# Queries stored beside the state: one product for keys by state and keys by queries in a delta-rule kernel

## The chip, the cores and the metric

The kernel runs on one core of one Trainium2 chip. The metric is the device time of one execution in microseconds, and the median of several executions is compared. Below, PE is TensorE (PEld its weight loads), DVE is VectorE, ACT is ScalarE, POOL is GpSimd and SP is SyncE.

## The reference

The kernel computes a linear attention with the delta rule, and feeds its result to a feed-forward layer with a PReLU whose slope differs by channel. There are B = 4 batches, H = 8 heads, S = 768 positions and a head size of D = 48; the feed-forward layer has 3072 tokens, a width of 384 and an inner width of 2048. All of it is fp32.

```python
k_n = k / (norm(k, axis=-1) + 1e-06)
state = zeros((B, H, D, D))
for t in range(S):
    kt, vt, bt = k_n[:, :, t], v[:, :, t], beta[:, :, t, None]
    y[:, :, t] = einsum('bhd,bhde->bhe', q[:, :, t], state)
    v_old = einsum('bhde,bhd->bhe', state, kt)
    state = state + bt[..., None] * einsum('bhd,bhe->bhde', kt, vt - v_old)
x = y.transpose(0, 2, 1, 3).reshape(B * S, H * D)
h = x @ w_in
g = maximum(h, 0.0) + alpha * minimum(h, 0.0)
out = g @ w_out
```

## The kernel before

**Chunks and steps.** Positions are taken in chunks of C = 64. A step n is one chunk for two of the four batches, so there are 12 x 2 = 24 steps, and steps n and n+2 belong to the same two batches and to the same state tile `state[bp]`. Within a chunk the recurrence is written as a triangular system. A step needs these products, each as 16 small matmuls, one for every combination of head pair g (4), head parity a (2) and batch t (2), in the order that `quarters()` gives:

- `grams(n_k, n_q)`: keys by keys for a later step n_k (L386, the triangular matrix), or keys by queries for step n_q (L386, then the mask `minus` on VectorE at L403, which gives `a_t`).
- `through_state(n)`: keys by state and queries by state (L672), both into one PSUM tile. VectorE subtracts the first from the scaled values (L675, the right-hand side `r`), ACT copies the second (L680, `y`).
- `between_1`, `between_2` (L629, L644): the off-diagonal block of the inverse.
- `solve(n)` (L686): inverse by right-hand side, scaled on VectorE (L690, `u`).
- `outputs(n)` (L699): `a_t` by `u`, added to `y` on VectorE (L706).
- `next_state(n)` (L715): keys by `u`, subtracted from the state by two VectorE instructions (L721).
- `flips` (L353) transposes keys and queries on TensorE, and ACT copies them to `k_t` and `q_t` (L375). `to_ffn` (L730, L732) transposes `y` for the feed-forward layer.

The operands of one small matmul lie in one half of the partitions (`dims(a)`: 48 rows from 0 or 64), and its output goes to one half of the PSUM partitions, so the four combinations of a and t use the four quarters of the array.

**Other work on VectorE.** The inverse of the 32-wide diagonal blocks is made by elimination for four steps at a time (L463 to L476, and transposes at L446). It is woven into the steps n with n % 4 < 3, as long as n < 20. The feed-forward layer needs L829 (ACT) and L831 (two VectorE instructions) for each bank of its first product, and sums of operands (L773) for a fast form of its second product (`ffn_out_fast`, L883).

**Order.** The instruction order of every engine is written out by hand. `weave` advances several generators in proportion to their lengths. From step 4 on, one step is `attention(n)` with four shares, between which matmuls of the feed-forward layer of an earlier chunk are placed (L819, first product; L883, second product):

1. `place(n+1)`, `through_state(n)`, `between_1(n+1)`
2. `solve(n)`, the key grams of step n+8, `between_2(n+1)`, scaling of v
3. `outputs(n)`, `next_state(n)`, the query grams of step n+1, loads
4. `flips` (keys of step n+9, queries of step n+2), `to_ffn(n)`, loads

Steps 0 and 1 have no state yet; `queries()` makes their query products. Steps 2 and 3 run together in `ready(2)` and `pair(2)`: there the query grams of both come in `ready`, and the state products of both stand back to back in `pair`. Step 4 is prepared by `prelude`.

**PSUM.** `ps_big()` hands out tiles of two banks from a ring of three. A request waits until every reader of the tile handed out three requests earlier is done. Two further banks (`p_ffn`) alternate for the feed-forward layer.

Of the kernel before, what the change touches and what calls it, by code (L numbers as in the profile page):

```python
# [25 lines left out]
FP32 = mybir.dt.float32  # L26
# [15 lines left out]
def kernel(  # L42
# [29 lines left out]
    def ps_big():  # L72


        return psum.tile([128, 2, 512], FP32, name="p_big", tag="big", bufs=3)
# [215 lines left out]
        nc.tensor.transpose(p, al_sb, ident[:FT, :FT])  # L291
        nc.scalar.activation(al_t, p, ACT.Copy, scale=-1.0, bias=1.0)

    state = [const.tile([128, 2, G, D], FP32, name=f"state{bp}") for bp in range(NB)]

    NE = 2
    diag = [const.tile([128, H, C], FP32, name=f"diag{i}") for i in range(NE)]
# [61 lines left out]
    def flips(n_k, n_q):  # L359

        both = n_k < N and n_q < N
        p = ps_big() if both else None
        copies = []
        if n_k < N:
            p_k = p[:, 0] if both else ps_one()
            flip(early(n_k), p_k)
            k_t[n_k] = work.tile([128, G, 128], FP32, name="k_t", bufs=EARLY + 1)
            copies.append((k_t[n_k], p_k))
        if n_q < N:
            p_q = p[:, 1] if both else ps_one()  # L370
            flip(q_pad[n_q % NQ], p_q)
            q_t[n_q] = work.tile([128, G, 128], FP32, name="q_t")
            copies.append((q_t[n_q], p_q))
        for dst, src in copies:
            nc.scalar.copy(dst.rearrange("p g i -> p (g i)"), src)  # L375

    def quarters():
        return [(g, a, t) for g in range(G) for a in range(2) for t in range(2)]

    def grams(n_k, n_q):  # L380

        p = ps_big().rearrange("p a (w g i) -> p a w g i", w=2, g=G)
        for w, n, rhs in ((0, n_k, k_t), (1, n_q, q_t)):
            if n < N:
                for g, a, t in quarters():
                    nc.tensor.matmul(  # L386
                        p[half(t ^ a if w else t), a, w, g], k_t[n][dims(a), g, half(t)],
                        rhs[n][dims(a), g, half(t)],
                    )
        if n_k < N:  # L390
            w = stats[n_k][1][:, 0:2, :, None].to_broadcast([128, 2, G, HB])
            for dst, cols in (
                (gather(n_k), slice(0, HB)), (right[n_k % EARLY][:, 1:], slice(HB, C))
            ):
                nc.vector.tensor_tensor(  # L395
                    out=dst.rearrange("p (a g) i -> p a g i", a=2), in0=p[:, :, 0, :, cols],
                    in1=w, op=ALU.mult,
                )
            keep(n_k)

        if n_q < N:
            a_t[n_q] = work.tile([128, H, C], FP32, name="a_t")
            nc.vector.tensor_tensor(  # L403
                out=a_t[n_q].rearrange("p (a g) i -> p a g i", a=2), in0=p[:, :, 1],
                in1=minus[:, None, None, :].to_broadcast([128, 2, G, C]), op=ALU.mult,
            )

# [253 lines left out]
    def through_state(n):  # L663
        c, bp = steps[n]
        if c == 0:
            rhs_[n] = by_parity(nv[n])
            return
        r = work.tile([128, H, D], FP32, name="r")
        p = ps_big()[:, :, 0 : 2 * G * D].rearrange("p a (w g d) -> p a w g d", w=2, g=G)
        for w, x in ((0, k_t), (1, q_t)):  # L670
            for g, a, t in quarters():
                nc.tensor.matmul(  # L672
                    p[half(t), a, w, g], x[n][dims(a), g, half(t)], state[bp][dims(a), t, g]
                )
        nc.vector.tensor_tensor(  # L675
            out=r.rearrange("p (a g) d -> p a g d", a=2), in0=by_parity(nv[n]), in1=p[:, :, 0],
            op=ALU.subtract,
        )
        y = work.tile([128, H, D], FP32, name="y")
        nc.scalar.copy(by_parity(y), p[:, :, 1])  # L680
        rhs_[n], ys[n] = r.rearrange("p (a g) d -> p a g d", a=2), y

    def solve(n):
        p = ps_big()[:, :, 0 : G * D].rearrange("p a (g d) -> p a g d", a=2, g=G)
# [271 lines left out]
    def attention(n):  # L956


        place(n + 1, (0,))
        through_state(n)  # L960
        between_1(n + 1)
        yield
        solve(n)
        grams(n + EARLY, N)
        between_2(n + 1)
        scale_v(n + 1)
        yield
        outputs(n)
        next_state(n)
        grams(N, n + 1)  # L970
        load_late(n + 2)
        squares(n + EARLY + 1)
        yield
        flips(n + EARLY + 1, n + 2)
        to_ffn(n)
        weigh(n + EARLY + 1)
        load_early(n + EARLY + 1 + NKE)
        load_q(n + 3)
        load_v(n + 3)
        yield  # L980
# [34 lines left out]
    def ready(n):  # L1015

        both = (n, n + 1)
        for i in both:
            place(i, (0,))
            flips(N, i)  # L1020
            load_q(i + 2)
        yield
        for i in both:
            between_1(i)
        yield
        for x in (1, 2, 3):
            for i in both:
                place(i, (x,))
        for i in both:
            grams(N, i)  # L1030
        yield
        for i in both:
            between_2(i)
            scale_v(i)
            yield

    def queries():

        p = [x.rearrange("p (n g i) -> p n g i", n=2, g=G) for x in ffn_banks]
        for n in range(2):  # L1040
            for g, a, t in quarters():
                nc.tensor.matmul(
                    p[a][half(t ^ a), n, g], k_t[n][dims(a), g, half(t)],
                    q_t[n][dims(a), g, half(t)],
                )
            a_t[n] = work.tile([128, H, C], FP32, name="a_t")

        def mask(n):
            for a in range(2):
                nc.vector.tensor_tensor(  # L1050
                    out=a_t[n][:, a * G : (a + 1) * G], in0=p[a][:, n],
                    in1=minus[:, None, :].to_broadcast([128, G, C]), op=ALU.mult,
                )

        return mask
# [48 lines left out]
    def statics(first, last):  # L1104
        if first > 0:
            squares(first)
        for n in range(first, last + 1):
            if n < last:
                squares(n + 1)
            weigh(n)  # L1110
            flips(n, N)
            yield
            if n > 0:
                load_early(n + NKE)
            if n > first:
                grams(n - 1, N)
            yield
        grams(last, N)
        yield


# [99 lines left out]
    def prelude(n):  # L1221
        place(n)
        yield
        between_1(n)
        yield
        between_2(n)
        yield
        grams(N, n)
        scale_v(n)
        yield  # L1230

    def catch_up():
        for n in range(FIRST + NJ, EARLY + NJ):
            grams(n, N)
            flips(n + 1, N)
            squares(n + 1)
            yield
            weigh(n + 1)
            load_early(n + 1 + NKE)
            yield  # L1240
# [65 lines left out]
```

## Time and profile before

| What | Value |
|---|---|
| Median of 5 runs | 686.56 us (686.35 to 687.33) |
| The profiled execution | 686.98 us, of it a span of 685.1 us in the profile |
| TensorE busy | 665.5 us (97%), 10063 matmul records |
| TensorE weight loads | 573.7 us (84%) |
| VectorE busy | 462.2 us (67%), 1133 instructions |
| ScalarE busy | 248.7 us (36%), 592 instructions |
| DMA | 37.76 MB, mean 55 GB/s |
| Granted TensorE clock | 0.999 |

The state products (L672) have 704 + 704 records, that is 22 steps of 16 + 16 matmuls with two records each; the query grams (L386) have 704. The records of a matmul overlap with those of its neighbours, so the time of a group is read from the start of the group to the start of the next one, not from the mean duration. Step n's state products start at 80.15 us for the pair of steps 2 and 3, at 155.54 for step 4, 170.17 for 5, 186.21 for 6, 214.48 for 7, and then every 25 to 26 us, until 619.26 for step 23. After 642 us only the feed-forward layer of the last chunk is left.

In a line of the timeline the columns are: start, duration, engine, line and operation, output and inputs, number of instructions merged, and in brackets the idle time before it with what ended it.

### The profile page before, as it was taken

How to read it: one execution, taken by the hardware profiler on the slowest of the kernel's cores; microseconds unless marked ns; L12 is line 12 of the kernel's file. 1: busy time of each engine (PE TensorE's matmuls, PEld its weight loads, DVE VectorE, ACT ScalarE, POOL GpSimd, SP SyncE). 2: the span in 40 equal slices, each digit the busy share in tenths (PEclk: the TensorE clock that was granted, in tenths of full speed). 3: DMA queues.
4: the chain of work that ended last, by engine and by line, in shares of the span. 5: the costliest groups of instructions: out<-in, count | busy, mean ns of one | idle time of the engine just before them, and what ended most of it. 6: DMA issues, size and time to landing. Idle time of an engine off the chain costs nothing.

```text
span 685.1 us, 22945 instructions
## 1 busy us (share of the span) xinstructions
PE 665.5 (97%) x10063; PEld 573.7 (84%) x10063; DVE 462.2 (67%) x1133; ACT 248.7 (36%) x592; POOL 19.3 (3%) x74
## 2 busy tenths in 40 slices
PE   6999999999999999999999999999999999999997
PEld 4567877666678988988988988988989989989997
DVE  5875799879988378967368967369877255245261
ACT  5936756334434244234234234134034133131110
POOL 4000010000000000000000000000000000000000
PEclk9999999999999999999999999999999999999999
DMA  8857654211412212212211111211211211100000
GB/s 126 223 142 204 164 106 117 69 36 35 81 28 40 41 36 45 40 35 47 39 35 37 36 26 36 38 26 34 48 22 28 54 24 20 35 3 2 24 1 23
DMA packets 110963, 37.76 MB, mean 55 GB/s; under 512 B 104160, under 2 KB 107248, under 8 KB 110864
## 3 DMA queue, kind: packets, MB, share of 16 engines
q1 hardware_dynamic: 109088, 35.81, 23.9%
q8 instruction: 79, 1.29, 0.8%
q10 hardware_dynamic: 1776, 0.49, 0.4%
q14 instruction: 20, 0.16, 0.1%
HBM read 31.56 MB, written 4.72 MB: 53 GB/s over the span
## 4 chain that ended last, share of the span: by engine, by line
PE 81%; DVE 11%; ACT 4%; issue 1%; DMA 1%; ACTq 0%; SPq 0%; DVEq 0%
PE p_ffn L819 33%; PE p_ffn L883 27%; PE p_big L672 3%; PE p_big L386 2%; PE p_big L353 2%; PE p_big L699 2%; PE p_big L686 2%; PE p_big L629 2%; PE p_big L989 2%; DVE block L476 2%; DVE prod L470 2%; PE p_big L644 1%; DMA ke<-in_k_dram 1%; PE p_big L715 1%; PE p_ffn L861 1%
## 5 line engine op out<-in xcount | busy, mean ns | idle before, releaser
L819 PE MATMUL p_ffn<-xt,w_in 128*128 128x256 f32 x1152 | 268.8, 385 | 5.1 <-DVE act L831 2.1
L819 PEld LDWEIGHTS p_ffn<-xt,w_in 128*128 128x128 f32 x1152 | 211.7, 190 | 35.9 <-issue 3.2
L831 DVE SCALAR_TENSOR_TENSOR act<-act,al_t,p_ffn 128x256 f32<-128x256 f32 x176 | 76.3, 475 | 70.8 <-ACT act L829 70.4
L829 ACT ACTIVATE act<-p_ffn 128x512 f32<-128x512 f32 x88 | 52.3, 595 | 124.4 <-PE p_ffn L819 124.2
L883 PE MATMUL p_ffn<-w_out,act 128*128 128x192 f32 x480 | 83.7, 328 | 0.0
L883 PEld LDWEIGHTS p_ffn<-w_out,act 128*128 128x128 f32 x480 | 78.6, 190 | 0.9
L476 DVE TENSOR_TENSOR block<-block,prod 128x30 f32<-128x30 f32 (+9 forms) x150 | 49.8, 332 | 5.2
L470 DVE TENSOR_TENSOR prod<-block 128x30 f32<-128x30 f32 (+9 forms) x150 | 48.8, 325 | 2.0
L903 DVE TENSOR_TENSOR o_sb<-u,p_ffn 128x192 f32<-128x192 f32 x40 | 13.2, 352 | 41.6 <-PE p_ffn L883 35.3
L680 ACT COPY y<-p_big 128x384 f32<-128x384 f32 x22 | 10.5, 479 | 69.6 <-DVE r L675 69.6
L375 ACT COPY q_t<-p_big 128x512 f32<-128x512 f32 x24 | 13.9, 590 | 55.8 <-PE p_big L353 55.8
L375 ACT COPY k_t<-p_big 128x512 f32<-128x512 f32 x24 | 13.9, 578 | 54.4 <-PE p_big L353 54.4
L883 PE MATMUL p_ffn<-space_out,sums 128*128 128x192 f32 x160 | 29.3, 326 | 0.0
L883 PE MATMUL p_ffn<-more,sums 128*128 128x192 f32 x160 | 29.3, 326 | 0.0
L883 PE MATMUL p_ffn<-w_out,sums 128*128 128x192 f32 x160 | 27.7, 326 | 0.0
L883 PEld LDWEIGHTS p_ffn<-more,sums 128*128 128x128 f32 x160 | 26.6, 190 | 0.0
L883 PEld LDWEIGHTS p_ffn<-space_out,sums 128*128 128x128 f32 x160 | 26.6, 190 | 0.0
L594 ACT ACTIVATE diag<-inverse,which 64x128 f32<-64x128 f32 (+2 forms) x62 | 25.4, 412 | 2.0 <-DVE inverse L446 1.2
L883 PEld LDWEIGHTS p_ffn<-w_out,sums 128*128 128x128 f32 x160 | 25.8, 190 | 0.0
L434 ACT COPY same<-right 32x256 f32<-32x256 f32 x32 | 12.9, 403 | 34.6 <-DVE right L395 34.4
L721 DVE TENSOR_TENSOR state<-state,p_big 48x384 f32<-48x384 f32 x44 | 24.1, 549 | 1.3 <-PE p_big L715 0.9
L903 DVE TENSOR_TENSOR u<-u,p_ffn 128x192 f32<-128x192 f32 x20 | 7.0, 352 | 25.4 <-PE p_ffn L883 25.4
(155 smaller groups left out, 948.2 us busy)
## 6 DMA issues: line engine op xcount, KB each, us to landing
w_out<-in_moe_w_in_dram SPq DMA_DIRECT2D x12, 512.0 KB, 4.6
qp<-in_q_dram SPq DMA_DIRECT2D x48, 96.0 KB, 3.0
v_raw<-in_v_dram SPq DMA_DIRECT2D x48, 96.0 KB, 3.3
kl<-in_k_dram SPq DMA_DIRECT2D x96, 48.0 KB, 2.4
out_dram<-o_sb SPq DMA_DIRECT2D x92, 48.0 KB, 1.6
space_out<-in_moe_w_out_dram SPq DMA_DIRECT2D x11, 384.0 KB, 4.2
ke<-in_k_dram SPq DMA_DIRECT2D x43, 96.0 KB, 3.1
w_out<-in_moe_w_out_dram SPq DMA_DIRECT2D x5, 384.0 KB, 4.5
```

The lines of the kernel that those rows point to most:

```text
L353: nc.tensor.transpose(p[:, g * 128 : (g + 1) * 128], src[:, 2 * g : 2 * g + 2].rearrange("p h d -> p (h d)"), ident,)
L375: nc.scalar.copy(dst.rearrange("p g i -> p (g i)"), src)
L470: nc.vector.tensor_tensor(out=prod, in0=r[:, 0:j, j : j + 1].to_broadcast([128, j, n]), in1=r[:, j : j + 1, j + 1 : HB].to_broadcast([128, ...
L476: nc.vector.tensor_tensor(out=r[:, 0:j, j + 1 : HB], in0=r[:, 0:j, j + 1 : HB], in1=prod, op=ALU.add)
L594: nc.scalar.mul(dst[n % NE][to or rows, a.start * G : a.stop * G, cols], src[m][rows, heads], which[rows, i : i + 1],)
L672: nc.tensor.matmul(p[half(t), a, w, g], x[n][dims(a), g, half(t)], state[bp][dims(a), t, g])
L721: nc.vector.tensor_tensor(out=x, in0=x, in1=p[dims(a)], op=ALU.subtract)
L819: nc.tensor.matmul(p_h[:, i], w_in[:, t, (f + i) * 128 : (f + i + 1) * 128], xt[:, t], start=(t == 0), stop=(t == KT - 1),)
L829: nc.scalar.activation(g, p_h, ACT.Relu, scale=-1.0)
L831: nc.vector.scalar_tensor_tensor(out=g[:, i], in0=g[:, i], scalar=al_t[:, f + i : f + i + 1], in1=p_h[:, i], op0=ALU.mult, op1=ALU.add,)
L883: nc.tensor.matmul(p, x(i), w(i), start=(i == 0), stop=(i == FP - 1))
L903: nc.vector.tensor_tensor(out=to, in0=x, in1=p, op=ALU.add)
```

## The change

The transposed queries of a step no longer have a tile of their own (`q_t`, two buffers in rotation). They are stored next to the state that they will meet: `beside[bp]` holds for every t and g the 48 state columns and then the 64 query columns. One product of the keys with these 112 columns gives both keys by state and keys by queries. The queries by state stay a product of their own, in a PSUM tile of its own. The odd heads' part of the combined product comes out in the other half of the partitions, as the masked `a_t` needs it, so the subtraction for `r` is made of three instructions: one for the even heads, and two for the odd heads, each of which reads one half of the partitions in PSUM and writes the other half. The mask follows it in `through_state`; the query grams at the end of the step before, in `ready` and in `prelude` are gone.

```diff
-    state = [const.tile([128, 2, G, D], FP32, name=f"state{bp}") for bp in range(NB)]
+    beside = [const.tile([128, 2, G, D + C], FP32, name=f"beside{bp}") for bp in range(NB)]
+    state = [x[:, :, :, 0:D] for x in beside]
 ...
 def flips(n_k, n_q):
-            q_t[n_q] = work.tile([128, G, 128], FP32, name="q_t")
-            copies.append((q_t[n_q], p_q))
+            q_t[n_q] = beside[steps[n_q][1]][:, :, :, D : D + C]
         for dst, src in copies:
             nc.scalar.copy(dst.rearrange("p g i -> p (g i)"), src)
+        if n_q < N:
+            nc.scalar.copy(
+                q_t[n_q].rearrange("p t g i -> p g t i"),
+                p_q.rearrange("p (g t i) -> p g t i", g=G, t=2),
+            )
 ...
-    def grams(n_k, n_q):
+    def grams(n):
     # the keys' part as before, in half of a buffer; the queries' part is gone, its mask is now:
+    def masked(n, p):
+        a_t[n] = work.tile([128, H, C], FP32, name="a_t")
+        nc.vector.tensor_tensor(
+            out=a_t[n].rearrange("p (a g) i -> p a g i", a=2), in0=p,
+            in1=minus[:, None, None, :].to_broadcast([128, 2, G, C]), op=ALU.mult,
+        )
 ...
 def through_state(n):
-        r = work.tile([128, H, D], FP32, name="r")
-        p = ps_big()[:, :, 0 : 2 * G * D].rearrange("p a (w g d) -> p a w g d", w=2, g=G)
-        for w, x in ((0, k_t), (1, q_t)):
-            for g, a, t in quarters():
-                nc.tensor.matmul(
-                    p[half(t), a, w, g], x[n][dims(a), g, half(t)], state[bp][dims(a), t, g]
-                )
-        nc.vector.tensor_tensor(
-            out=r.rearrange("p (a g) d -> p a g d", a=2), in0=by_parity(nv[n]), in1=p[:, :, 0],
-            op=ALU.subtract,
-        )
+        p = ps_big()[:, :, 0 : G * (D + C)].rearrange("p a (g e) -> p a g e", g=G)
+        for g, a, t in quarters():
+            nc.tensor.matmul(
+                p[half(t ^ a), a, g], k_t[n][dims(a), g, half(t)], beside[bp][dims(a), t, g]
+            )
+        p_y = ps_big()[:, :, 0 : G * D].rearrange("p a (g d) -> p a g d", g=G)
+        for g, a, t in quarters():
+            nc.tensor.matmul(
+                p_y[half(t), a, g], q_t[n][dims(a), t, g], state[bp][dims(a), t, g]
+            )
+        r = work.tile([128, 2, G, D], FP32, name="r")
+        v_in = by_parity(nv[n])
+        for to, own, a in (
+            (slice(0, 128), slice(0, 128), 0), (half(0), half(1), 1), (half(1), half(0), 1)
+        ):
+            nc.vector.tensor_tensor(
+                out=r[to, a], in0=v_in[to, a], in1=p[own, a, :, 0:D], op=ALU.subtract
+            )
+        masked(n, p[:, :, :, D : D + C])
         y = work.tile([128, H, D], FP32, name="y")
-        nc.scalar.copy(by_parity(y), p[:, :, 1])
+        nc.scalar.copy(by_parity(y), p_y)
 ...
 def attention(n):
-        grams(n + EARLY, N)
+        grams(n + EARLY)
 ...
-        grams(N, n + 1)
 def ready(n):
-        for i in both:
-            grams(N, i)
 def prelude(n):
-        grams(N, n)
```

## The prediction

> **What bounds the kernel now.** I read the page's span, busy shares and chain first, then the busy time by stretches.
>
> ```profile
> span 685.1 us, 22945 instructions
> ...
> PE 81%; DVE 11%; ACT 4%; issue 1%; DMA 1%; ACTq 0%; SPq 0%; DVEq 0%
> ```
> ```profile
> core 0: us, PE busy (x) PEld busy (x) DVE busy (x) ACT busy (x) POOL busy (x), PEclk, DMA share, GB/s
> 78.00:104.00 26.00, 23.60 (x500) 18.32 (x496) 23.64 (x59) 15.07 (x33) 2.21 (x4) 1.00 0.56 139
> ...
> 157.00:213.00 56.00, 52.75 (x965) 39.86 (x965) 50.69 (x127) 23.96 (x62) 2.46 (x8) 1.00 0.26 49
> 213.00:642.00 429.00, 428.55 (x6410) 392.05 (x6411) 276.24 (x653) 131.93 (x318) 3.47 (x16) 1.00 0.16 32
> ```
>
> There are two regimes. From 213 to 642 us, steps 7 to 23, TensorE has work for 428.55 of 429 us: a saving there reaches the end in full, and VectorE costs something only where TensorE waits for it. Before 213 us TensorE and VectorE are both over 90% busy in the stretches that hold steps 2, 3 and 5, 6, and the chain of waits runs largely through VectorE: a TensorE saving there is worth little, and VectorE's extra work counts. So the change has to be costed twice.
>
> The price of a group of 16 small products comes from the timeline of TensorE in step 12, and that of a column from the chain's last two pieces.
>
> ```profile
> 350.29 0.68 PE L686 MATMUL p_big<-r,inv 64*64 64x48 f32 x32
> 350.79 0.66 PE L386 MATMUL p_big<-k_t 48*64 48x64 f32 x32
> 351.27 0.62 PE L644 MATMUL p_big<-diag,mid 64*64 64x32 f32 x32
> ```
> ```profile
> 642.49 20.72 PE p_ffn L819 x96
> 663.21 18.21 PE p_ffn L883 x112
> ```
>
> Sixteen products are 32 records. A group with 64 columns starts the next one after 0.48 us; in step 13 one with 48 takes 0.47 (the query group of L672 starts at 369.61, L629 at 370.08). The pitch hardly depends on the columns, while 64x48 weights (L715) bring it to 0.36: loading weights sets it. The full array takes 20.72/96 = 216 ns for 256 columns and 18.21/112 = 163 ns for 192, so 0.83 ns a column and 3 ns fixed.
>
> VectorE's prices and its slack come from the groups by form and the timelines of steps 2, 3 and 9.
>
> ```profile
> L403 DVE TENSOR_TENSOR a_t<-p_big,minus 128x512 f32<-128x512 f32 x22 | 15.1, 691 | 0.5
> L903 DVE TENSOR_TENSOR o_sb<-o_sb,p_ffn 128x192 f32<-128x192 f32 x10 | 3.5, 354 | 16.2 <-PE p_ffn L883 16.2
> ```
> ```profile
> 81.58 0.65 PE L672 MATMUL p_big<-state,q_t 48*64 48x48 f32 x32
> 82.16 1.56 PE L819 MATMUL p_ffn<-xt,w_in 128*128 128x256 f32 x6
> 82.22 1.01 DVE L675 TENSOR_TENSOR r<-v_raw,p_big 128x384 f32<-128x384 f32 x2
> 82.80 0.94 ACT L680 COPY y<-p_big 128x384 f32<-128x384 f32 x2 [3.21 <-DVE r L675]
> 85.31 0.88 DVE L831 SCALAR_TENSOR_TENSOR act<-act,al_t,p_ffn 128x256 f32<-128x256 f32 x2 [1.81 <-ACT act L829]
> ```
> ```profile
> 268.01 0.55 DVE L675 TENSOR_TENSOR r<-v_raw,p_big 128x384 f32<-128x384 f32 x1
> 269.39 2.76 PE L883 MATMUL p_ffn<-w_out,act 128*128 128x192 f32 x16
> 270.98 0.87 DVE L831 SCALAR_TENSOR_TENSOR act<-act,al_t,p_ffn 128x256 f32<-128x256 f32 x2 [0.36 <-ACT act L829]
> ```
>
> Consecutive VectorE operations start closer than they last: L675 to the next start is 0.47 us (268.01 to 268.47), a 256-wide L395 takes 0.34 and L403 takes 0.61. That is about 1.04 ns an element, so a 192-wide piece should cost 0.27. Three pieces cost 0.82 where one cost 0.47: +0.35 us of VectorE a step. With the mask behind them, 1.43 us stand together where 0.47 stood.
>
> **A. TensorE, steps 7 to 23.** Removed: the gram group of the queries at the end of a step (0.47; for steps 8 to 23 it lies in this stretch, 16 times) with its PSUM buffer. The group of keys by state grows from 48 to 112 columns. No row has 112 columns in a quadrant. Below, the pitch stays 0.47, if only weights count. Above, it grows with the columns from the 64-column row: 0.48 x 112/64 = 0.84. The full array's price per column gives 0.83 x 112 + 3 = 96 ns a record, and four quadrants alongside make eight rounds: 0.77. For 64 columns the same sum gives 0.45, just under the 0.48 seen, which is why the columns do not show yet. I take 0.77, +0.30 for each of 17 steps. A = 17 x 0.30 - 16 x 0.47 = -2.4 us; with the ends -7.5 and -1.2.
>
> The Trainium skill (TensorE: Matmul & The Clock Gate, Back-to-back issue gap, and Measured speedup vs the span model) lets a product stream a column per 2.4 GHz cycle, N/2.4 + 2.5 ns, and tiles beside it add some 4 ns each. An estimate from that page is 8 x (49 + 12) = 0.49 us, nearly free, and A would be near -7. The rows show 0.83 ns a column and record for these fp32 operands, twice the page's figure, so the rows decide.
>
> **B. Steps 9, 13 and 17.** Odd steps run the first fast output product right after the state products, and its eighth weight load needs the first L831. In step 9 that load is due at 269.39 + 14 x 0.163 - 0.19 (a load's duration) = 271.48, and L831's first half ends at 271.46: no slack. After: VectorE is 0.95 later, less its 0.36 idle, so 272.06; the product is due 0.30 later, 271.78. A stall of 0.28 and some 0.06 of signalling, 0.34 us, in the three odd steps where elimination fills VectorE: B = +1.0 (0 to +1.5). In the other odd steps VectorE idles 1.82 us before that L831 (321.76), in even ones 2.14 (297.32); these cover the 0.95 there, and without them it would cost the same 0.34.
>
> **C. Steps 2 and 3, taken together.** Both run the state products back to back. Before they took two PSUM buffers, now four, from a ring of three. So the second query product of step 3 waits until step 2's subtractions and mask have been read: 82.22 + 0.82 + 0.69 = 83.73, where TensorE is ready at 82.2. Queued behind it on TensorE are that product, six records of L819 and the solve of step 2; ACT's copy of y, the evacuation L829 and VectorE's L831 wait for these. L819 then starts at about 84.35 instead of 82.16. TensorE has only the 0.35 us wait of the later transposes to give back, and VectorE, 1.9 us longer (2 x 0.35, and two masks of 0.61 that leave a stretch ruled by ACT near 73 us), loses its idle 1.81 too. The later TensorE waits at 100 us (0.94) and 104 us (1.43) are for VectorE, which by then is as late. C = +1.9 (0.1 if only VectorE's work counts, 2.2 in full).
>
> **D. Steps 4 to 6.** In step 4 the chain is on TensorE and holds the gram group: -0.48. From 170 to 206 us it is on VectorE: two steps at +0.35; step 5's mask comes onto the chain (+0.61), that of step 7 leaves it (-0.61). ACT's copy of y waited for the subtraction since both read one PSUM buffer; now it reads its own, so L829 no longer sits behind it and VectorE's idle 0.56 before L831 at 193.06 goes. D = -0.48 + 0.70 - 0.56 = -0.3 (-1.0 to +0.8).
>
> **At nothing.** ACT's copy of the queries keeps its 512 elements; permuted ACT outputs such as L732 cost no more (490 against 479 ns). It now writes beside the state, so it may wait for L721; in step 12 L721 ends at 359.5 and the copy starts at 365.05, 5.5 us of cover. Queries for step n+2 overwrite those of step n, read four phases earlier. No DMA moves: the SyncE queue keeps its order, and GpSimd's too. The masks still finish a phase before their use in L699; without that cover a late one would cost its 0.69.
>
> The Trainium skill (VectorE: DVE Perf Modes, The TRN2 errata) speaks against this change: every instruction pays a fixed share, so small pieces pay it again. Its fp32 tensor_tensor formula, (N+151)/0.96 ns, gives 357 ns for 192 elements (here 354), and if starts were that far apart three pieces would cost +0.51 instead of +0.35; over the eight steps of B, C and D that is an estimated +1.3 us. The starts in the timeline are closer than the durations, so I keep 0.35.
>
> **Sum.** -2.4 + 1.0 + 1.9 - 0.3 = +0.2 us. The profiled execution took 686.98 us (span 685.1 and 1.9 around it), 0.42 above the median of 686.56. So 687.2 against its own time, and 686.8 where a median is measured. About 0.2%, 1.4 us, is what a measurement of this kernel can tell from no change.
>
> **Rivals.** *Wide products are free (faster).* The group stays at 0.47: A = -7.5; the output product is then due 0.30 earlier, so B = +1.9. With C and D it is -4.0, 682.6 us. For it: the pitch did not move between 32 and 64 columns. Against: 0.83 ns a column leaves no more room at 64. *VectorE's pieces do not overlap (slower).* If the three subtractions and the mask start a full duration apart (0.354 and 0.69), a step costs 0.32 more: B +1.0, C +0.6, D +0.6, in all +2.4, 689.0 us. It decides from about 0.17 more a step. For it: the pieces read another partition half than they write, which no row shows. Against: every other pair of VectorE operations overlaps. *The early stall is absorbed.* C = 0.1 gives -1.6, 685.0, just beyond the bound on the fast side.
>
> **Chances.** Forecast, no measurable change: 0.38. Free wide products 0.18 and an absorbed early stall 0.10 make faster 0.28. VectorE's pieces 0.20, and 0.14 for the upper ends of A, B and C together (A -1.2, B 1.5, C 2.2: +2.2), make slower 0.34. The forecast's own range is 685.4 to 688.0. The range for 8 in 10 goes from the free products, 682.6, to the slower rival with A's upper end half counted, 689.5.
>
> **What would show it.** The group of keys by state and queries should start the next one after 0.77 us, with every other group where it was. Between 213 and 642 us the stretch should be 1 to 2 us shorter, with TensorE waits below 0.5 us in steps 9, 13 and 17. TensorE should stand still for about 1.5 us inside the state products near 82 us. ACT's 69.6 us of waiting for r should be gone. A pitch of 0.5, a gap missing at 82 us, or VectorE starts 0.35 apart within the subtraction would each prove one term wrong.

## The result, and the profile after

The changed kernel takes 686.18 us (median of 52 runs), the kernel before 686.83 (95 runs beside them): a ratio of 0.9991, interval 0.9984 to 0.9997. It is faster by some 0.6 us, where +0.2 was forecast. That is less than the 1.4 us that the prediction called measurable, but the many runs separate it from nothing. The profiled execution took 685.77 us. Below, "lag" is the start of a feed-forward record after, less the start of the same record before (negative is ahead).

The page's span and chain of waits:

```profile
span 683.9 us, 21599 instructions
...
PE 79%; DVE 13%; ACT 4%; DMA 2%; issue 2%; ACTq 0%; SPq 0%; DVEq 0%
```

VectorE's share of the chain rose from 11% to 13%, TensorE's fell from 81% to 79%. Busy time by stretches (start:end, length, then busy us and instructions of each engine, granted clock, DMA share, GB/s):

```profile
core 0: us, PE busy (x) PEld busy (x) DVE busy (x) ACT busy (x) POOL busy (x), PEclk, DMA share, GB/s
78.00:104.00 26.00, 22.78 (x454) 17.88 (x453) 25.37 (x65) 14.57 (x33) 2.20 (x4) 1.00 0.46 116
157.00:213.00 56.00, 51.66 (x869) 38.92 (x869) 51.23 (x129) 24.04 (x61) 2.27 (x7) 1.00 0.25 48
213.00:642.00 429.00, 428.05 (x5906) 390.74 (x5905) 287.66 (x691) 134.36 (x318) 3.48 (x16) 1.00 0.16 32
```

The two regimes are still there. VectorE is busy 25.37 of 26 us around the pair of steps 2 and 3 (23.64 before), and TensorE still 428.05 of 429 from 213 us on. The lag by stretch:

| Stretch | Lag at its start and end | Change | Forecast |
|---|---|---|---|
| to 50 us (same instructions) | 0, -0.68 | -0.68 | 0 |
| 50 to 95 us, steps 2 and 3 | -0.68, -0.14 | +0.54 | C = +1.9 |
| 95 to 202 us, steps 4 to 6 | -0.14, +0.46 | +0.60 | D = -0.3 |
| 202 to 620 us, steps 7 to 23 | +0.46, -1.24 | -1.70 | A + B = -1.4 |

The 0.68 us at the start isn't the change: the profiled executions of the kernels below, which run the same instructions there, were between 0.47 us early and 3.13 late at 50 us. The other three rows add up to -0.56, close to what the medians say.

TensorE's timeline in step 13 (start, duration, what ran, number of records):

```profile
368.92 1.00 PE L675 MATMUL p_big<-beside,k_t 48*64 48x112 f32 x32
369.73 0.63 PE L680 MATMUL p_big<-beside 48*64 48x48 f32 x32
370.18 0.63 PE L634 MATMUL p_big<-diag,right 64*64 64x32 f32 x32
...
375.20 0.59 PE L897 MATMUL p_ffn<-w_out,act 128*128 128x192 f32 x2 [0.18 <-DVE act L845]
```

The group with 112 columns starts the next one after 0.81 us, where 0.77 was estimated. The two products together take 1.26, against 0.97 before (369.11 to 370.08), so the forecast +0.30 is there. The last line is one of the stalls of term B: the lag rises by 0.45 there, and by 0.45 in step 9. Step 17 has none.

The chain in the same step shows VectorE's part (start, duration, operation):

```profile
370.98 0.27 DVE r L689
371.26 0.36 DVE r L689
371.63 0.35 DVE r L689
371.98 0.03 issue
372.01 0.69 DVE a_t L408
```

The third piece starts 0.37 after the second, and the mask 0.38 after that; the prediction had 0.27 for each piece. (The chain counts the first piece only from the end of the instruction before it.) In the timelines below, from the first piece to the mask it is 1.09 us (81.50 to 82.59) and 1.15 (190.36 to 191.51). Forecast was 0.82.

The pair of steps 2 and 3, timeline of the three engines:

```profile
79.96 0.48 ACT L694 COPY y<-p_big 128x384 f32<-128x384 f32 x1 [1.07 <-PE p_big L680]
...
80.53 1.00 PE L675 MATMUL p_big<-beside,k_t 48*64 48x112 f32 x32 [0.65 <-DVE right L399]
...
81.32 0.66 PE L680 MATMUL p_big<-beside 48*64 48x48 f32 x32
81.50 1.08 DVE L689 TENSOR_TENSOR r<-v_raw,p_big 128x192 f32<-128x192 f32 x3
...
82.59 0.69 DVE L408 TENSOR_TENSOR a_t<-p_big,minus 128x512 f32<-128x512 f32 x1
...
85.17 0.87 DVE L845 SCALAR_TENSOR_TENSOR act<-act,al_t,p_ffn 128x256 f32<-128x256 f32 x2
```

Step 3's query product starts at 81.32, before step 2's first subtraction (81.50) and mask (82.59). The stop of 1.5 us inside the state products doesn't happen. TensorE does stop for a PSUM tile, but earlier and for less: 0.65 us before step 3's first product (80.53). It waits for L399 there, whose output the product doesn't use; the tile is what it waits for, the one of the key grams that L399 reads. L845 follows without the 1.81 us of idle time that VectorE had there before.

Step 6, timeline, and ACT's wait for the state products from the waits of the whole run (total, times, longest):

```profile
190.01 0.32 DVE L481 TENSOR_TENSOR block<-block,prod 128x150 f32<-128x150 f32 x1
190.36 1.12 DVE L689 TENSOR_TENSOR r<-v_raw,p_big 128x192 f32<-128x192 f32 x3
191.51 0.69 DVE L408 TENSOR_TENSOR a_t<-p_big,minus 128x512 f32<-128x512 f32 x1
...
199.54 0.67 PE L833 MATMUL p_ffn<-xt,w_in 128*128 128x256 f32 x2 [1.70 <-DVE prod L475]
```
```profile
ACT y L694 <- PE p_big L680: 57.3, 21, 5.5
```

ACT no longer waits for `r` (69.6 us before), as forecast. But TensorE waits 1.70 us for the elimination at 199.54, where it waited 0.98 before: VectorE is later.

### The profile page after: what moved, and what is told of

The parts are those of the page before. It is cut to its first block, busy times and chain, and to the rows that moved or that the text cites. A ratio compares the mean times of both kernels' runs of the same rounds, so it can differ in the third digit from the quotient of the medians.

```text
span 683.9 us, 21599 instructions
## 1 busy us (share of the span) xinstructions
PE 660.7 (97%) x9359; PEld 569.7 (83%) x9359; DVE 475.1 (69%) x1177; ACT 251.3 (37%) x592; POOL 19.3 (3%) x74
## 4 chain that ended last, share of the span: by engine, by line
PE 79%; DVE 13%; ACT 4%; DMA 2%; issue 2%; ACTq 0%; SPq 0%; DVEq 0%
PE p_ffn L833 32%; PE p_ffn L897 27%; PE p_big L355 2%; DVE block L481 2%; PE p_big L675 2%; DVE prod L475 2%; PE p_big L713 2%; PE p_big L700 2%; PE p_big L1002 2%; PE p_big L634 2%; DVE act L845 1%; PE p_big L392 1%; PE p_big L649 1%; DMA ke<-in_k_dram 1%; PE p_big L680 1%
## 5 line engine op out<-in xcount | busy, mean ns | idle before, releaser
L845 DVE SCALAR_TENSOR_TENSOR act<-act,al_t,p_ffn 128x256 f32<-128x256 f32 x176 | 76.4, 475 | 56.2 <-ACT act L843 55.3
L378 ACT COPY beside<-p_big 128x512 f32<-128x512 f32 x24 | 13.9, 589 | 54.2 <-PE p_big L355 52.3
L689 DVE TENSOR_TENSOR r<-v_raw,p_big 64x192 f32<-64x192 f32 (+1 forms) x66 | 23.2, 352 | 7.3 <-PE p_big L675 6.2
```

The lines of the kernel that those rows point to most:

```text
L378: nc.scalar.copy(q_t[n_q].rearrange("p t g i -> p g t i"), p_q.rearrange("p (g t i) -> p g t i", g=G, t=2),)
L689: nc.vector.tensor_tensor(out=r[to, a], in0=v_in[to, a], in1=p[own, a, :, 0:D], op=ALU.subtract)
L845: nc.vector.scalar_tensor_tensor(out=g[:, i], in0=g[:, i], scalar=al_t[:, f + i : f + i + 1], in1=p_h[:, i], op0=ALU.mult, op1=ALU.add,)
```

## The experiments

Two theories stood against each other after the result. Theory: steps 7 to 23 gain as forecast; VectorE's pieces are slower than forecast because each is held until the one before it has ended; the first steps lose by VectorE's work alone. Rivals: the pieces are slow because they have 64 partitions; the early steps lose by PSUM or by TensorE's order; the start of the run decides. Each run has the kernel before beside it.

**One subtraction.** Leaves out the swap of the halves for the odd heads, so all of VectorE's added piece cost goes and nothing else.

```diff
-        for to, own, a in ((slice(0, 128), slice(0, 128), 0), (half(0), half(1), 1), (half(1), half(0), 1)):
-            nc.vector.tensor_tensor(out=r[to, a], in0=v_in[to, a], in1=p[own, a, :, 0:D], op=ALU.subtract)
+        nc.vector.tensor_tensor(out=r, in0=v_in, in1=p[:, :, :, 0:D], op=ALU.subtract)
```

> The changed kernel with one subtraction over both halves of the partitions instead of three; it leaves out the exchange of halves for the odd heads. Theory (pieces that start in another half do not overlap, so the three cost 1.12 us of VectorE instead of 0.47): 0.65 us less VectorE in every step; steps 5 and 6 give back 1.3 us, the TensorE stalls of 0.45 us in steps 9 and 13 vanish (0.9), the pair of steps 2 and 3 gives up to 0.6: 2.2 us below the changed kernel (1.6 to 2.8), ratio to the kernel before about 0.996. Rival (the mask that moved to the start of the step is what hurts, not the pieces): under 0.6 us below the changed kernel, ratio 0.9983 or more.

Measured: 683.64 us, ratio 0.9948 (0.9930 to 0.9966), 2.5 us under the changed kernel by the medians (3.0 by the ratios). The sixteen products of step 13 that stalled now run in one piece:

```profile
370.83 2.76 PE L892 MATMUL p_ffn<-w_out,act 128*128 128x192 f32 x16
```

So the pieces cost the change some 2.5 us, and term B is theirs. The lag tells where the rest is: in steps 4 to 6 it falls by 0.72 instead of rising by 0.60, so 1.3 us are the pieces' there. In the pair it still rises by 0.35, of 0.54 with the pieces: only 0.2 us of the pair's loss is theirs.

**The form of the pieces.** The subtraction takes a different form in each step n, by n % 4; forms 1 to 3 leave out the swap. Form 0 is the change's own, form 1 keeps both halves where they are, form 2 is two whole-width pieces and form 3 the single instruction.

```diff
+        every, lo, hi = slice(0, 128), half(0), half(1)
+        if n % 4 == 3:
+            nc.vector.tensor_tensor(out=r, in0=v_in, in1=p[:, :, :, 0:D], op=ALU.subtract)
         for to, own, a in (
-            (slice(0, 128), slice(0, 128), 0), (half(0), half(1), 1), (half(1), half(0), 1)
-        ):
+            ((every, every, 0), (lo, hi, 1), (hi, lo, 1)),
+            ((every, every, 0), (lo, lo, 1), (hi, hi, 1)),
+            ((every, every, 0), (every, every, 1)),
+            (),
+        )[n % 4]:
```

> The changed kernel with four forms of the subtraction in turn, by step number modulo 4; forms 1 to 3 leave out the exchange of halves for the odd heads. 0: as the change has it (whole, low from high, high from low). 1: whole, low from low, high from high. 2: two whole pieces, even and odd heads. 3: one instruction. Theory (an instruction waits for the end of the one before it when an operand starts in another half than that one's): starts 0.35 to 0.39 apart for every piece of form 0 and to the mask; in form 1 whole to low 0.27, low to high and high to mask 0.35 or more; in form 2 0.27 and 0.27; in form 3 0.47 to the mask. Rival (64-partition pieces are slow in themselves): form 1 has 0.35 or more everywhere after its first piece starts, and whole to low in form 1 is as in form 0.

Only the trace of its one execution (685.66 us) is read. VectorE's timeline in one step of each form, in the order 0, 1, 2, 3:

```profile
242.19 1.12 DVE L695 TENSOR_TENSOR r<-v_raw,p_big 128x192 f32<-128x192 f32 x3 [0.60 <-PE p_big L675]
243.35 0.69 DVE L408 TENSOR_TENSOR a_t<-p_big,minus 128x512 f32<-128x512 f32 x1
...
268.23 0.97 DVE L695 TENSOR_TENSOR r<-v_raw,p_big 128x192 f32<-128x192 f32 x3
269.23 0.69 DVE L408 TENSOR_TENSOR a_t<-p_big,minus 128x512 f32<-128x512 f32 x1
...
293.71 0.62 DVE L695 TENSOR_TENSOR r<-v_raw,p_big 128x192 f32<-128x192 f32 x2 [0.60 <-PE p_big L675]
294.25 0.68 DVE L408 TENSOR_TENSOR a_t<-p_big,minus 128x512 f32<-128x512 f32 x1
...
318.84 0.55 DVE L688 TENSOR_TENSOR r<-v_raw,p_big 128x384 f32<-128x384 f32 x1 [0.32 <-PE p_big L675]
319.31 0.68 DVE L408 TENSOR_TENSOR a_t<-p_big,minus 128x512 f32<-128x512 f32 x1
```

From the first start to the mask's start: 1.16, 1.00, 0.54 and 0.47 us. Taken apart record by record, starts in form 0 are 387, 387 and 381 ns apart; in form 1 264, 354 and 388; in form 2 271 and 265. A piece of half the partitions that begins in the same half as the one before it follows after 264 ns, as quickly as a whole one; whatever changes the half waits out the full duration. The size of the pieces is no cause; the change of half is. The Trainium skill (VectorE: DVE Perf Modes, Two Vector instructions with no wait between them) has this as a rule: an instruction whose input or output begins in another partition quadrant than the last one's in the same memory starts only when every earlier one has finished. The four forms agree with it; the prediction drew on that page's formula and missed this section.

**The pieces in the kernel before.** Only the odd heads' keys-by-state product goes to the other half, and `r` is made of three pieces; query grams and masks stay.

```diff
-                    p[half(t), a, w, g], x[n][dims(a), g, half(t)], state[bp][dims(a), t, g]
+                    p[half(t if w else t ^ a), a, w, g], x[n][dims(a), g, half(t)],
+                    state[bp][dims(a), t, g],
...
-        nc.vector.tensor_tensor(
-            out=r.rearrange("p (a g) d -> p a g d", a=2), in0=by_parity(nv[n]), in1=p[:, :, 0],
-            op=ALU.subtract,
-        )
+        v_in = by_parity(nv[n])
+        for to, own, a in (
+            (slice(0, 128), slice(0, 128), 0), (half(0), half(1), 1), (half(1), half(0), 1)
+        ):
+            nc.vector.tensor_tensor(
+                out=r[to, a], in0=v_in[to, a], in1=p[own, a, 0], op=ALU.subtract
+            )
```

> The kernel before with one thing changed: the odd heads' part of the keys-by-state product comes out in the other half of the partitions, and the subtraction is made of the three pieces. The query grams, their masks and TensorE's work stay. Theory (a piece that starts in another half is held for the one before it, 0.38 us apart): 0.65 us more on VectorE a step; in steps 2 and 3 VectorE's idle 1.81 us takes it, in steps 5 and 6 it is on the path (2 x 0.65), in steps 9, 13 and 17 0.65 less 0.36 idle makes a stall of about 0.3 each: +2.2 us in all, a ratio of 1.0032. Rival (the prediction's price, starts overlap, 0.35 more a step): 0.7 in steps 5 and 6 and nothing in the odd steps, +0.7 us, 1.0010.

Measured: 690.77 us, ratio 1.0056 (1.0044 to 1.0069), +3.9 us, more than the theory's 2.2. The lag tells where: +1.26 in the pair, +1.32 in steps 5 and 6, +0.54, +0.54 and +0.13 in steps 9, 13 and 17. (The profiled execution, 691.74 us and so 1.0 over the median, also loses 0.84 near 70 us and 0.52 in step 11, where TensorE waits 0.52 and 0.26 for "issue".) Steps 5 and 6 are as the theory had them, and steps 9 and 13 lose more than its 0.3 each. The pair isn't the theory's at all: VectorE's idle time there was not free.

```profile
82.75 2.24 DVE L680 TENSOR_TENSOR r<-v_raw,p_big 128x192 f32<-128x192 f32 x6
83.96 0.48 ACT L684 COPY y<-p_big 128x384 f32<-128x384 f32 x1 [3.83 <-DVE r L680]
85.08 0.48 ACT L684 COPY y<-p_big 128x384 f32<-128x384 f32 x1 [0.64 <-DVE r L680]
...
87.11 0.48 DVE L835 SCALAR_TENSOR_TENSOR act<-act,al_t,p_ffn 128x256 f32<-128x256 f32 x1 [1.73 <-ACT act L833]
```

The products are done at 82.7, but ACT copies `y` only when the pieces have read the tile that it shares with them. ACT's evacuation then comes later and VectorE waits for it as long as ever (1.73). In the changed kernel `y` has its own tile and the copy runs at 79.96, so the same pieces fall into that idle time. With the own tile the pieces cost the pair 0.2 us, as the single subtraction showed, and without it 1.26.

**A tile for y alone.** In the kernel before, the queries-by-state product gets a PSUM tile of its own; nothing else changes.

```diff
-        p = ps_big()[:, :, 0 : 2 * G * D].rearrange("p a (w g d) -> p a w g d", w=2, g=G)
+        p, p_y = (ps_big()[:, :, 0 : G * D].rearrange("p a (g d) -> p a g d", g=G) for _ in range(2))
```

> The kernel before with the queries by state in a PSUM tile of its own, so that ACT's copy of y no longer waits for the subtraction; no other part of the change. Theory (TensorE-bound after 213 us, and before that ACT's wait costs VectorE its 0.56 us idle near 193 us): 0.3 to 0.6 us below the kernel before, ratio 0.9992 to 0.9996. Rival (the third buffer per step makes TensorE wait for PSUM in the pair of steps 2 and 3): slower, ratio 1.001 or more.

Measured: 687.18 us, ratio 1.0002 (0.9985 to 1.0018): no gain is seen, but the interval holds the expected one and the rival's loss. The trace has both: the lag falls by 0.64 in steps 4 to 6 (+0.23 at 152 us, -0.41 at 199), which is the -0.56 of term D; but it rises by 0.59 in the pair (-0.38 to +0.21), where two more tiles are asked for. Of this, 0.35 is there right behind the state products, and 0.33 comes in step 3's solve, whose products take 1.01 us instead of 0.68 for no reason that the profile shows. The profiled execution also has a hiccup of 3.4 us that no other profile has in this size:

```profile
320.21 0.24 PE L629 MATMUL p_big<-diag,right 64*64 64x32 f32 x2 [1.46 <-issue]
```
```profile
core 0: us, PE busy (x) PEld busy (x) DVE busy (x) ACT busy (x) POOL busy (x), PEclk, DMA share, GB/s
...
322.00:324.00 2.00, 2.00 (x6) 1.58 (x5) 0.00 (x0) 0.00 (x0) 0.00 (x0) 0.50 0.00 0
```

TensorE stands 1.46 us for nothing that the profile shows, and the granted clock is 0.50 behind it. Its lag is therefore read up to 307 us only.

**The product split.** The 112 columns as one product of 48 and one of 64.

```diff
+        for cols in (slice(0, D), slice(D, D + C)):
             for g, a, t in quarters():
                 nc.tensor.matmul(
-                    p[half(t ^ a), a, g], k_t[n][dims(a), g, half(t)], beside[bp][dims(a), t, g]
+                    p[half(t ^ a), a, g, cols], k_t[n][dims(a), g, half(t)], beside[bp][dims(a), t, g, cols]
```

> The changed kernel with its 112-column product made as two, 48 state columns and then 64 query columns, into the same PSUM tile; all else is the same. Theory (112 columns cost 0.80 us a group, 48 and 64 cost 0.47 and 0.48): +0.15 us in each of the 17 steps from step 7 on, +2.6 us above the changed kernel less what the stalls of steps 9 and 13 absorb (0.3), ratio to the kernel before about 1.002 to 1.003. Rival (wide columns are nearly free, a group costs 0.5): +7 us.

Measured: 689.95 us, ratio 1.0034 (1.0013 to 1.0055), 3.0 us over the changed kernel by the ratios (3.8 by the medians). In step 13:

```profile
371.63 1.16 PE L676 MATMUL p_big<-beside,k_t 48*64 48x48 f32 x64
372.62 0.63 PE L682 MATMUL p_big<-beside 48*64 48x48 f32 x32
```

The two groups take 0.99 us where the joined one took 0.81: 0.18 a step, 3.1 us in 17 steps. So the joined product saves 0.18 us a step and is neither free nor without use. The expected ratio lies inside the interval; the profiled execution also has a stop of TensorE in step 11, "issue" again (0.56 at 321.94).

**The mask moved.** The mask is recorded at the start of `solve`, behind whatever VectorE is given between.

```diff
-        masked(n, p[:, :, :, D : D + C])
+        late_mask[n] = p[:, :, :, D : D + C]
...
 def solve(n):
+        if n in late_mask:
+            masked(n, late_mask.pop(n))
```

> The changed kernel, with the mask of a step recorded at the start of its solve instead of right behind the subtractions, one share of the weave later. Theory: L831's successor (L845 there) comes 0.6 us earlier in steps 9 and 13, their TensorE stalls fall from 0.45 us to under 0.1, the VectorE-bound steps 5 and 6 are unchanged since the work is the same: 0.9 us below the changed kernel (0.6 to 1.2), ratio to the kernel before 0.998. Rival (mask hurts in the early steps too): 1.5 us or more below. If the buffer that the mask holds longer makes TensorE wait before the solve or the grams, it is slower than the changed kernel.

Measured: 705.24 us, ratio 1.0273 (1.0248 to 1.0298): far off the gain that was expected. What the expectation named last, TensorE waiting for the buffer, is what came. (The profiled execution took 709.14 us.)

```profile
285.54 0.68 DVE L408 TENSOR_TENSOR a_t<-p_big,minus 128x512 f32<-128x512 f32 x1
...
286.27 1.08 PE L649 MATMUL p_big<-diag,mid 64*64 64x32 f32 x32 [3.20 <-DVE a_t L408]
```

The mask now stands behind elimination and sums in VectorE's order, and it holds its PSUM tile until then; `between_2` waits 3.20 us for that tile. So the ring of three does bite, but by the last reader's place in VectorE's order, and where the change put the mask, no wait of TensorE for it shows.

**The change from step 7 on.** Steps 2 to 6 keep the old products, subtraction, query grams and masks (the queries still lie beside the state).

```diff
+    SPLIT = 7
...
+        if n < SPLIT:            # the old through_state, on beside's columns
...
+            return
...
         next_state(n)
+        asked(n + 1)             # the old query grams and mask, for 2 <= n < SPLIT
```

> The changed kernel from step 7 on; steps 2 to 6 make the query grams a step ahead and the two state products apart, as before. Theory (by stretch, the change costs 0.5 us in steps 2 and 3 and 0.6 in steps 4 to 6, and gains 1.7 after 213 us): 1.7 us below the kernel before, ratio 0.9975, 1.1 below the changed kernel. Rival (the grams that are gone from the early steps pay for the pieces there): as the changed kernel, ratio 0.999.

Measured: 684.94 us, ratio 0.9971 (0.9954 to 0.9988), as the theory had it. The lag is -0.44 at 50 us, -0.51 at 199 and -2.72 at the end. The first steps are where the change loses.

**The same with the mask moved.**

> Both edits together: the change from step 7 on only, and its mask at the start of the solve. Theory: the two gains add, 1.1 + 0.9 below the changed kernel, 2.6 below the kernel before (1.9 to 3.2), ratio 0.9962. Rival: one of them is not there, ratio 0.9975 or more.

Measured: 698.64 us, ratio 1.0166 (1.0146 to 1.0187). It fails in the same way: `between_2` waits for the mask 5 times, 9.9 us in all.

**The query grams of steps 2 and 3 made once more.** To the changed kernel, the two groups and masks that it took out of `ready` are added again; they compute nothing new.

```diff
+        for i in both:
+            p = ps_big()[:, :, 0 : G * C].rearrange("p a (g i) -> p a g i", g=G)
+            for g, a, t in quarters():
+                nc.tensor.matmul(p[half(t ^ a), a, g], k_t[i][dims(a), g, half(t)], q_t[i][dims(a), t, g])
+            masked(i, p)
```

> The changed kernel with the query grams of steps 2 and 3 and their masks made once more in their old place, before the pair; the second result is the one that is used. Theory (the pair costs little because TensorE arrives 1.2 us earlier when these grams are gone): TensorE is back to the old time near 73 us, and the end is 0.5 to 1.2 us above the changed kernel. Rival (ACT rules that stretch anyway, and the pair is cheap only because the second query product got another buffer): under 0.3 us above.

Measured: 686.43 us, ratio 0.9975 (0.9952 to 0.9997), no slower than the changed kernel: the theory fails, its rival holds. The added groups stand in the trace:

```profile
71.91 1.16 PE L1045 MATMUL p_big<-beside,k_t 48*64 48x64 f32 x64
```

One microsecond of TensorE before the pair is worth nothing. The saving of those two groups never reached the end.

**The change up to step 6 only.** As "from step 7 on", with the two conditions turned round.

```diff
-        if n < SPLIT:
+        if n >= SPLIT:
```

> The combined product in steps 2 to 6 alone; from step 7 on the state products, the single subtraction and the query grams are those of before. Theory (VectorE is the engine that sets these steps, and its four pieces cost 0.6 us more a step than the one subtraction): the terms C and D alone, measured as +0.54 and +0.6 us by the two traces, less nothing later: +1.1 us, a ratio of 1.0016 to before. Rival one (the 0.7 us by which the changed kernel starts earlier belongs to the change, or TensorE's saved group in these steps reaches the end): 0 or a gain, ratio at most 1.000. Rival two (the prediction's own terms, a strict ring of PSUM buffers): +1.6 us with TensorE standing still inside the state products of the pair, ratio 1.0023.

Measured: 688.53 us, ratio 1.0026 (1.0014 to 1.0037), +1.8 us. A gain in the early steps is excluded. The expected 1.0016 lies inside the interval, and so does the third figure, 1.0023; between these two the trace decides (its profiled execution came to the pair 3 us late, so only differences are read). The lag rises by 0.6 from 50 to 95 us, and by 1.0 from there to 202.

```profile
84.35 1.00 PE L705 MATMUL p_big<-beside,k_t 48*64 48x112 f32 x32 [0.64 <-DVE right L399]
...
85.14 0.66 PE L710 MATMUL p_big<-beside 48*64 48x48 f32 x32
85.32 1.08 DVE L719 TENSOR_TENSOR r<-v_raw,p_big 128x192 f32<-128x192 f32 x3
```

Again the query product starts before the first piece: no stop for the mask.

**From step 7 on, without steps 9 and 13.** These two, the ones that stalled, stay on the old way as well.

```diff
-        if n < SPLIT:
+        if n < SPLIT or n in ODD:      # ODD = (9, 13)
```

> As the kernel that has the combined product from step 7 on only, but with steps 9 and 13, the two in which TensorE was seen to wait, left in the old way. Theory (the stall there is VectorE's longer series of pieces ahead of the PReLU): each of the two steps loses its saving on TensorE of 0.18 us and its stall of 0.34, so 0.3 us faster than that kernel, a ratio of 0.9967 to before against 0.9971. Rival (the stall comes from the elimination and stays): 0.35 us slower than that kernel, 0.9976. The difference is near what can be resolved; the trace decides, by whether TensorE waits before the second product of steps 9 and 13.

Measured: 684.32 us, ratio 0.9961 (0.9948 to 0.9973). Beside "from step 7 on" the ratios can't tell the two apart, but the trace shows the stall of step 9 gone (all 16 in one piece), so it was the combined step's and not the elimination's (and the pieces', as the single subtraction shows):

```profile
268.55 2.76 PE L927 MATMUL p_ffn<-w_out,act 128*128 128x192 f32 x16
```

It is the fastest version here that leaves nothing out, 1.9 us faster than the changed kernel by the medians and 2.7 faster than the one before by its ratio. The single subtraction, which leaves out the swap, marks how much more the pieces still hold back: 0.9948.

## Why the prediction was wrong, and where it was right

**A, TensorE in steps 7 to 23: right.** Forecast -2.4. The products measured +0.30 a step and each removed group 0.48, so 17 x 0.30 - 16 x 0.48 = -2.6. The price of 112 columns, worked out from 0.83 ns a column, was 0.77 and came as 0.81. The rival "wide products are free" falls, and with it the 0.49 that the prediction estimated from the page on TensorE.

**B, the stalls: cause right, sizes off, sum right.** Forecast 0.34 in each of steps 9, 13 and 17; measured 0.45 in two, in all 0.9 against 1.0. The stall is the pieces': with one subtraction there is none, with the pieces alone it is 0.54. The pieces are 0.3 us longer than forecast; why only 0.11 of that shows isn't worked out. Step 17 isn't like step 9: before, its L675 starts 0.01 after the first product's L819 (472.40 and 472.39), in step 13 0.45 after (371.09 and 370.64), so VectorE had 0.44 to spare there. One step was read for three.

**C, the pair: the step that failed.** Forecast +1.9, measured +0.54. It rested on a strict ring, in which a request waits for the readers of the tile three requests back. That is what the section on PSUM above says too, and it doesn't hold as said. Step 3's query product went ahead at 81.32, when the tile of step 2's combined product was still to be read (81.50 to 83.28) and that of step 3's was just being filled. There are three tiles, so it can only have been given the third, the one of step 2's `y`, which ACT had copied by 80.44 (79.96 + 0.48): a free tile, not the oldest. The gap that the prediction named as a sign is missing.

What the runs show in its place: TensorE's wait of 0.65 for the tile of the key grams, which the sum didn't have, and then VectorE. Right behind the pair's products, the lag is 0.43 above that at 50 us, and 0.44 with the single subtraction. From there on the single subtraction ends the pair at +0.35 and the pieces at +0.54. VectorE's sum comes close to that: with the pieces as measured, 2 x (1.09 - 0.47) + 2 x 0.61 = 2.46 more, less the 1.81 of idle time, is 0.65. So the lower end, "only VectorE's work counts" (0.1), was nearer, but it lacked TensorE's wait and the held pieces. That the idle time could be used at all is due to `y`'s own tile, as the pieces alone show.

**D, steps 4 to 6: the price of the pieces.** Forecast -0.3, measured +0.6. The gram group gave its 0.48 (the lag falls from -0.15 to -0.63 at 165 us). The -0.56 for ACT's freed copy is supported by the tile for y alone (-0.64 there). The pieces cost 0.66 more in each of the two steps (1.32 in the pieces alone) instead of 0.35, which puts the sum at -0.48 + 1.32 - 0.56 = +0.3. Most of the other 0.3 is a term that the prediction didn't have. In steps 5 and 6 the first piece starts 0.43 and 0.35 after the instruction before it (190.01 to 190.36 above), where L675 started 0.31 and 0.23 after, before its predecessor had ended. Rows of VectorE for step 6 of the kernel before, and then the state update of step 5 in the changed kernel:

```profile
183.71 0.69 DVE L403 TENSOR_TENSOR a_t<-p_big,minus 128x512 f32<-128x512 f32 x1
...
189.83 0.32 DVE L476 TENSOR_TENSOR block<-block,prod 128x150 f32<-128x150 f32 x1
190.06 0.55 DVE L675 TENSOR_TENSOR r<-v_raw,p_big 128x384 f32<-128x384 f32 x1
```
```profile
183.35 1.11 DVE L735 TENSOR_TENSOR beside<-beside,p_big 48x384 f32<-48x384 f32 x2
```

The single subtraction has the same 0.43 and 0.35, so these 0.23 us are not the pieces'. They fit the change of half as well: the mask used to be the last to read PSUM before the subtraction, over all partitions. Now it is the second state update, which reads the upper half, and what runs between doesn't touch PSUM. In steps 5 and 6 the subtraction is held so in all seven kernels whose mask is gone from there, and in none of the six that still have it there (before, pieces alone, tile for y alone, and the three that change from step 7 on). TensorE shows all this at 199.54, in its longer wait for the elimination. The last 0.1 is near what step 7's mask, counted with -0.61, gave less: with it and its gram group gone the lag falls by 0.48 (+0.94 at 199 us, +0.46 at 202).

**The slower rival, pieces that don't overlap, was half right.** Its mechanism is what happens, and its price per step, +0.32 over the forecast's 0.35, is what was measured (0.62 to 0.68 in all). The prediction gave it 0.20 because "no row shows" a change of partition half. A row did: the two state updates L721 of the kernel before each write one half, and the chain has them, with what follows, a full duration apart.

```profile
93.45 0.54 DVE state L721
94.00 0.56 DVE state L721
94.59 0.42 DVE same L395
```

0.55 and 0.59 apart, where L675 of the same size is followed after 0.47. So "every other pair of VectorE operations overlaps" was a misreading. The figure was taken from the rows that overlap, not from the one that was like the new instruction. The sum still came out too slow by 0.8, because the strict ring had charged 1.4 us too much for the pair: two errors against each other, +0.9 in D, most of it VectorE's held instructions, and -1.4 in C. That the forecast came as near as 0.8 is luck. Those two and the -0.3 in A and B make the -0.8 between forecast and result.

## What to carry to other kernels

Before splitting an instruction of VectorE by partitions, look in the trace for a pair that changes halves in the same way and take its start-to-start time; the price of neighbours that stay in one half does not apply. When an instruction that reads PSUM is moved, look at which half the one now last before its successor reads. Cost a change once for each regime of the kernel, and if the regimes differ in sign, make it only where it pays: here the change from step 7 on is worth three times the whole. VectorE's idle time ahead of an instruction that waits for ACT is only free if ACT doesn't wait for the added work through a shared PSUM tile.

## What was not expected of the hardware

- VectorE instructions of 192 elements start some 264 to 272 ns apart as long as they begin in the same partition half, and 345 to 390 ns apart when they change it, the next whole-width instruction included. Instructions between that don't touch PSUM do not undo it: the subtraction of step 6 starts 0.35 us after a predecessor of 0.32 when PSUM was last read in the upper half, and 0.23 after it otherwise.
- Sixteen small products on the four quarters of the array have a pitch that hardly moves from 48 to 64 columns (0.45 to 0.50 us a group) and is 0.81 at 112. Where between them the columns begin to count, no run here shows.
- TensorE stood for 0.26 to 1.46 us in step 11, near 320 us, waiting for nothing that the profile shows ("issue"), in three kernels (split product, tile for y alone, pieces alone) and not there in the kernels before and after; in one of them a granted clock of 0.50 followed. A stop of the same kind, of 0.25 to 1.07, stands near 47 us in eleven of the thirteen profiles, the kernels before (0.52) and after (0.81) among them. No run here tells what brings it.
